# A fused attention and mixer kernel on one core: one group for the last 64 features, denser second sums, v weights on ScalarE's queue, a third band buffer, and a new order

## The chip, the core and the metric

The kernel runs on one core of a Trainium2 chip. A core has five engines that the text names as the profile does: TensorE (PE; PEld is its loading of weights), VectorE (DVE), ScalarE (ACT), GpSimd (POOL) and SyncE (SP). Each engine runs its own instructions strictly in the order in which the program gives them and waits on semaphores for the others. SP here only issues DMA transfers. The metric is the time of one execution on the device in microseconds (us), the median of several runs; less is better. The notes also use one profiled execution, whose span runs from its first to its last instruction.

## What is computed

The input x has 2048 tokens of 448 features. Two blocks follow each other, each on a layer-normalized input and each added to its input; all normalizations have no learned scale.

```python
h  = x + A(layernorm(x), wqkv, wo)
h2 = h + B(layernorm(h), w1, w2, w3, w4)

# A: 16 heads of 28 features; each token attends to itself and the
#    tokens 2, 4, ... 14 before it (8 in all), softmax over these 8
# B: g  = gelu(layernorm(x) @ w1), cut into four groups of 112 features,
#         shifted by +1, -1, +2, -2 tokens
#    x1 = x + g @ w2
#    return x1 + gelu(layernorm(x1) @ w3) @ w4      # w3: 448 -> 1792
```

## The kernel before

The tokens are worked on in four quarters of 512 (t = 0 to 3) and, from the mixer's second product on, in five units u of 2, 4, 4, 4 and 2 tiles of 128 tokens. The steps of a quarter are, with the names of the functions:

- N1 (line 654): statistics and normalization of x. VectorE makes most of it, ScalarE that of quarter 3.
- A1 (line 670): the normalized rows are transposed (by PE in quarters 0 and 1, by a DMA transpose in 2 and 3); then q and k of 3 x 128 features each and of the last 64 features (line 692). The copies out of PSUM (evictions) write `qT`, and `kk` or, for the last 64 features, `kr`, with 16 tokens of the stretch before as a pad in front.
- V (line 719): v, evicted to `vt`, spread by DMAs into bands `vw`.
- A2 (line 742): VectorE multiplies queries with eight shifted copies of the keys, 4096 columns for each of three feature groups and 2048 for the last 64 features ("products"); PE sums them over a head's features into logits.
- S (line 765): softmax over the eight: row maximum, difference, Exp, sum, Ln and Exp, multiplication into `pb`; PE turns `pb`, and the result is evicted to `pt`.
- A3 (line 791): VectorE spreads `pt` over a band `bd_r` (80 x 2048, "band product"), PE multiplies it with `vw`; then O (line 806): the product with wo and the residual.
- B1 (line 837): statistics, normalization, DMA transpose; M (line 850): the product with w1, gelu into `gT`.

The steps of a unit are B2 (line 868: the product with w2 over the shifted groups, "second sums"), T (line 905: normalization, transposes by PE in unit 0 and by DMA in the others), W3 (line 915) and B3 (line 932). W3 makes 14 groups of 128 features for each unit, with gelu on ScalarE, and B3 the product with w4 and the stores.

Most sums over features are made by `duo` (line 459): two outputs at a time, each summed over 64-row halves of the array's rows. At each step a matmul on rows 0 to 63 for one output and one on rows 64 to 127 for the other run as a pair. The function `sums` (line 482) gives one output four upper and three lower halves and the other three and four, so 448 features take seven pair steps ("3.5 passes" of full height an output).

The groups of the mixer have 112 features, so their lower half has only 48 rows. For units 0 and 1 (`DENSE = 2`, line 19) the second sums take four upper and four lower halves an output: eight pair steps. From unit 2 on, seven DMAs a unit (line 874) gather the lower rows densely into `ht`, with w2's rows in the same order in `w2_l` (seven loads, line 964), and seven pair steps do.

The last 64 features of q and k (lines 692 to 705) are summed in quarters of the array, 64 rows by 64 columns: X takes q and Y takes k, with the even tiles of a quarter in the upper 64 partitions of the output and the odd ones in the lower. These are 28 matmuls of 256 columns. Three pads (lines 713 to 716) are copied besides.

The order of the work is written out by hand in a list of numbers, `ORDER` (line 20). Each operation has a number in the order in which the code creates it; `arrange` (line 193) goes through the list, hands out buffers, and appends each operation to its engine's instructions. `OTHER` (line 52) names operations that go to VectorE in place of ScalarE. A transposing DMA waits for the landing of all ordinary DMAs that stand before it in the list, and an ordinary DMA for the transposing one before it (lines 206 to 211). The loads of an engine's queue keep their order (line 452). At the start PE runs `WARM = 11` matmuls on the identity (line 647).

Of the kernel before, what the change touches and what calls it, by code (L numbers as in the profile page):

```python
# [50 lines left out]
"""  # L51
OTHER = """
92 182 483 489 492 495 546 552
"""
FULL = (4,)
FILL = (0, 0, 0, 0)
WARM = 11
# [225 lines left out]
def bass_sequential_preLN__sliding_local_dilated__mixer_s_mlp__prompt_kernel(  # L283
# [18 lines left out]
    LOWER = ((0, 64, 112, 0, 64), (1, 64, 80, 0, 112), (1, 80, 112, 1, 64), (2, 64, 96, 1, 96), (2, 96, 112, 2, 64), (3, 64, 112, 2, 80), (3, 0, 64, 3, 64))  # L302
# [11 lines left out]
    with ExitStack() as es:  # L314
# [14 lines left out]
        w2_s = sb("w2_s", [KC, 4, D], BF16)  # L329
        w2_l = sb("w2_l", [128, 4, D], BF16)  # L330
        ht = sb("ht", [128, 4, 512], BF16)
# [35 lines left out]
        gT = arv(A_QG, KC, 4 * QGW).rearrange("p (c n) -> p c n", c=4)  # L367
        kk = [arv(A_KV + t * KVB, 128, 3 * KVW).rearrange("p (c n) -> p c n", c=3) for t in range(NST)]
        kr = [arv(A_KV + t * KVB + 3 * KVW, 128, 4 * KW).rearrange("p (j n) -> p j n", j=4) for t in range(NST)]
# [5 lines left out]
        def shifted(t, c):  # L375
            return bass.AP(AR, A_KV + t * KVB + c * KVW + PADK, [[A_END, 128], [64, 8] if c < 3 else [KW, 4], [-DIL, NW], [1, 64]])
# [50 lines left out]
        def load_x(i, n):  # L427
            return dma("x%d" % i, xin[:, i:i + n, :], xv[:, i:i + n, :], 128 * n * D * 2)

        def load_rows(chan, dst, src, lo, n):  # L430

            for h in range(2):
                dma("%s%s" % (chan, "ab"[h]), dst[:, 2 * h:2 * h + 2, :], src[192 * h:192 * h + 256, lo:lo + n].rearrange("(c k) n -> k c n", k=128), 256 * n * 2)
# [16 lines left out]
        dma("w2", w2_s[:], B_w2.rearrange("(c k) n -> k c n", k=KC), D * D * 2)  # L450
# [169 lines left out]
        def setup_late(after):  # L620
# [15 lines left out]
            late("memset", ap=kr[0][0:64, 0, 0:PADK], constant=0.0)  # L636
            late("memset", ap=vw[0:PADK, 0, 0, :], constant=0.0)
            late("memset", ap=gT[:, :, 0:2], constant=0.0)
            late("memset", ap=gT[:, :, 2 + SEQ:4 + SEQ], constant=0.0)
# [30 lines left out]
        def phase_A1(t):  # L670
# [37 lines left out]
            def last(lo, h, n):  # L708
                return Y(lambda v: v[64 * h:64 * h + 64, 0:256].rearrange("p (j n) -> p j n", j=4)[:, lo:lo + n, 64 - PADK:])
# [342 lines left out]
```

## Time and profile before

| | |
|---|---|
| median of 3 runs | 189.51 us (188.73 to 191.31) |
| span of the profiled execution | 186.4 us |
| what the median has around that span | 3.1 us |
| PE busy | 180.3 us, 2496 matmuls |
| VectorE busy | 127.0 us |
| ScalarE busy | 122.1 us |
| GpSimd busy | 24.0 us |
| DMA | 18.59 MB, of it 8.14 MB read from HBM |

The profile gives no time of the profiled execution outside of its span. Matmuls overlap, and their ends are modelled, so a busy PE can still contain short waits. Nearly every instruction has the line 1010, where the program emits what was recorded before; so groups are told apart by the names of what is written and read (`ps` is a bank of PSUM, `arena` the memory that q, k, gelu results and the weights wqkv, w3 and w4 share, `w_s` the weights w1 and w2). Times of points are microseconds from the start of the span.

### The profile page before, as it was taken

Reading aid. Unit: us, or ns where it says so; the run is one execution under the profiler, and the core shown is the slowest. Engines: PE = TensorE matmul, PEld = TensorE weight load, DVE = VectorE, ACT = ScalarE, POOL = GpSimd, SP = SyncE. Lnnn points to the kernel's source line nnn. Section 1 sums busy time; section 2 is a strip of 40 time slices with the busy share of each in tenths; the row PEclk is TensorE's granted clock in tenths of the full one; section 3 lists DMA queues with packets and bytes.
Section 4 is the critical chain, followed back from the end, with each engine's and each line's share of the span. In section 5 each row is a group of like instructions: output and inputs, shape, how many; then the busy total and the mean of one; then the engine's idle time right before and its main releaser. Section 6 shows DMA issues by size and latency. Waiting matters only on the chain.

```text
span 186.4 us, 5772 instructions
## 1 busy us (share of the span) xinstructions
PE 180.3 (97%) x2496; PEld 94.0 (50%) x2496; DVE 127.0 (68%) x225; ACT 122.1 (65%) x289; POOL 24.0 (13%) x59
## 2 busy tenths in 40 slices
PE   6899998999999999999999999999999999999994
PEld 2474333445544565765455544554445544555663
DVE  6799999999999999999476587614087274000403
ACT  3549999898999999957959489503833004730340
POOL 4320000000000000425300000170002805000000
PEclk9999999999999999999999999999999999999999
DMA  5999025865515667914360201491111602300121
GB/s 134 356 282 182 16 51 130 198 216 71 144 38 110 115 216 165 307 53 45 73 116 10 58 8 26 88 141 54 29 40 41 116 0 52 106 0 4 49 98 49
DMA packets 33633, 18.59 MB, mean 100 GB/s; under 512 B 21208, under 2 KB 33096, under 8 KB 33608
## 3 DMA queue, kind: packets, MB, share of 16 engines
q1 hardware_dynamic: 33608, 18.23, 41.5%
q8 instruction: 19, 0.31, 0.6%
q14 instruction: 6, 0.05, 0.1%
HBM read 8.14 MB, written 1.84 MB: 54 GB/s over the span
## 4 chain that ended last, share of the span: by engine, by line
PE 79%; DVE 14%; ACT 4%; DMA 1%; issue 0%; SPq 0%
PE ps L1010 79%; DVE qk_r L1010 9%; DVE st L1010 1%; ACT lntm L1010 1%; DMA xin<-in_A_x_dram 1%; DVE lntm L1010 1%; ACT L1010 1%; DVE mx L1010 1%; DVE xin L1010 1%; ACT arena L1010 1%; ACT h3T L1010 1%; DVE pb L1010 0%; DVE ls L1010 0%; DVE mv L1010 0%; ACT rs_x L1010 0%
## 5 line engine op out<-in xcount | busy, mean ns | idle before, releaser
L1010 PE MATMUL ps<-actT,arena 64*128 64x512 bf16 (+2 forms) x812 | 69.8, 326 | 0.9 <-DMA actT<-lntm 0.5
L1010 ACT ACTIVATE h3T<-ps 128x512 bf16<-128x512 f32 (+1 forms) x70 | 30.9, 517 | 38.5 <-PE ps L1010 38.4
L1010 PEld LDWEIGHTS ps<-actT,arena 64*128 64x128 bf16 (+1 forms) x812 | 35.4, 96 | 31.9 <-PE ps L1010 1.9
L1010 PE MATMUL ps<-arena,h3T 64*128 64x448 bf16 (+3 forms) x434 | 44.9, 343 | 0.2
L1010 ACT ACTIVATE arena<-ps 128x512 bf16<-128x512 f32 (+6 forms) x66 | 30.7, 508 | 8.5 <-PE ps L1010 8.1
L1010 PEld LDWEIGHTS ps<-arena,h3T 64*128 64x128 bf16 (+1 forms) x434 | 22.6, 94 | 20.0 <-ACT h3T L1010 0.6
L1010 DVE TENSOR_TENSOR qk_r<-arena 128x4096 bf16<-128x4096 bf16 (+1 forms) x16 | 31.9, 2013 | 0.1
L1010 DVE SCALAR_TENSOR_TENSOR qk_r<-ps,mrs,arena 128x448 bf16<-128x448 f32 (+2 forms) x17 | 10.4, 651 | 30.9 <-PE ps L1010 30.9
L1010 POOL TENSOR_TENSOR arena<-arena,xin 128x448 f32<-128x448 f32 x16 | 16.1, 1035 | 77.9 <-ACT lntm L1010 65.5
L1010 DVE TENSOR_TENSOR bd_r<-arena,bmask 80x2048 bf16<-80x2048 bf16 x16 | 19.0, 1214 | 1.7 <-PE ps L1010 1.7
L1010 DVE SCALAR_TENSOR_TENSOR arena<-xin,rs_y,ps 128x448 f32<-128x448 bf16 x16 | 10.3, 671 | 11.0 <-PE ps L1010 11.0
L1010 PE MATMUL ps<-wo_s,actT 64*128 64x448 bf16 x128 | 14.5, 350 | 0.1
L1010 PE MATMUL ps<-actT,w_s 64*112 64x512 bf16 x112 | 13.4, 379 | 0.0
L1010 PE MATMUL ps<-w_s,arena 64*128 64x448 bf16 x83 | 12.8, 349 | 0.1
L1010 PE MATMUL ps<-arena,actT 64*128 64x448 bf16 x112 | 12.3, 351 | 0.2
L1010 ACT ACTIVATE actT<-ps 128x512 bf16<-128x512 f32 (+2 forms) x19 | 11.7, 639 | 1.1 <-PE ps L1010 1.0
L1010 ACT ACTIVATE lntm<-xin,nm 128x448 bf16<-128x448 bf16 x16 | 10.6, 672 | 1.1 <-DVE nm L1010 1.1
L1010 DVE BATCH_NORM_STATS2 st<-xin 128x6 f32<-128x448 bf16 x16 | 9.2, 614 | 1.0 <-DMA xin<-in_A_x_dram 0.9
L1010 PEld LDWEIGHTS ps<-actT,w_s 64*112 64x112 bf16 x112 | 7.2, 126 | 4.4 <-ACT arena L1010 0.3
L1010 ACT ACTIVATE rs_x<-mv,epsilon 128x4 f32<-128x4 f32 (+2 forms) x16 | 4.6, 298 | 6.4 <-DVE mv L1010 6.3
L1010 PEld LDWEIGHTS ps<-w_s,arena 64*128 64x128 bf16 x83 | 5.5, 95 | 6.1 <-PE ps L1010 0.5
L1010 ACT ACTIVATE vt<-ps 128x448 bf16<-128x448 f32 x16 | 8.3, 546 | 0.5 <-PE ps L1010 0.5
(73 smaller groups left out, 161.6 us busy)
## 6 DMA issues: line engine op xcount, KB each, us to landing
arena<-in_B_w_dram SPq DMA_DIRECT2D x2, 896.0 KB, 5.9
out_dram<-qk_r SPq DMA_DIRECT2D x15, 112.0 KB, 1.8
arena<-in_B_w_dram SPq DMA_DIRECT2D x2, 784.0 KB, 7.3
vw<-vt SPq DMA_DIRECT2D x4, 320.0 KB, 4.3
vw<-vt SPq DMA_DIRECT2D x4, 256.0 KB, 4.1
arena<-in_A_wqkv_dram SPq DMA_DIRECT2D x2, 448.0 KB, 4.7
xin<-in_A_x_dram SPq DMA_DIRECT2D x2, 448.0 KB, 7.5
xin<-in_A_x_dram SPq DMA_DIRECT2D x3, 224.0 KB, 5.5
```

Of the source, the lines that this page charges most:

```text
L1010: inst = getattr(eng, meth)(**kw)
```

## The change

1. *Last 64 features.* A weight tile `wl` holds the last 64 features of q and of k beside each other; GpSimd copies it together once (`setup_last`). Each half of a quarter (256 tokens) is one output of 128 features, and a `duo` sums the two halves: 14 matmuls of 256 columns in the place of 28. The heads' tokens in `kr`, the logits, `pb` and `pt` are laid out by halves instead of even and odd tiles. Four copies of 64 partitions x 256 take the place of two of 128 x 256, and one pad copy that of two.
2. *Second sums.* All units use seven pair steps. Features 64 to 111 of the last group are split over rows 112 to 127 of the other three, by three DMAs a unit (`low`), and the odd tiles' first 64 features of the last group go to the lower half (`odd`, one DMA a unit). w2 is loaded in that arrangement by four loads; `w2_l` and its seven loads go.
3. *Loads.* The v weights are issued on ScalarE's queue and stand first in the list of its loads. On SP x4-5 goes ahead of the second half of the q and k weights.
4. *Buffers and start.* Three band buffers in place of two. Quarter 0's q and k take the 512 tokens in one piece, no longer in two of 256. `WARM` is 7, and one such matmul stands behind each of the first two transposes (`FILL`).
5. *Order.* `ORDER` and `OTHER` are new. What it says around the points that are spoken of here:
   - VectorE, ahead of quarter 0's first product: all four statistics and three aggregates of quarter 2's x (before, two statistics, and the others between the products); both reductions to `bmask` ahead of the first statistics.
   - ScalarE at the start: the v loads after the third transposition copy, then the evictions q0, k0, a row sum of tile 13, q1, k1, q2, k2, the two k halves, quarter 1's two transposition copies, four v evictions, the two q halves, an Ln and an Exp, the pad.
   - SP after quarter 1's DMA transpose: four DMAs of unit 0, one of v, four of unit 1, the second half of w3, w4. Before: the second half of w3, one of v, six of `w2_l`, two of v, w4.
   - PE: the phases follow each other much as before; within them many pairs are exchanged.

```diff
-NQK, NBD, NLN, NACT, NSM, NO = 3, 2, 2, 4, 1, 6
+NQK, NBD, NLN, NACT, NSM, NO = 3, 3, 2, 4, 1, 6
-DENSE = 2
 ORDER = """
-8 9 2 10 12 0 1 39 40 41 42 43 44 45 46 47 48 49 13 5 14 4 15 16 6 33 7 50 17 18 29 51 36 37 34 30 52 55 53 54 56 62
+32 2 36 5 33 8 0 39 6 35 9 1 10 14 15 16 34 43 44 45 17 7 18 50 55 51 52 19 53 46 62 56 60 47 57 48 54 49 63 58
...
-FILL = (0, 0, 0, 0)
-WARM = 11
+FILL = (1, 1, 0, 0)
+WARM = 7
...
+        for h in range(2):
+            load_half("wv", wqkv_s[:, :, 2 * D:3 * D], A_wqkv, 2 * D, D, h, "act")
         act(zs[:, 0, 0:1], epsilon[:, 0:1], ACT.Exp)
-        load_rows("wqk", wqkv_s[:, :, 0:2 * D], A_wqkv, 0, 2 * D)
+        load_half("wqk", wqkv_s[:, :, 0:2 * D], A_wqkv, 0, 2 * D, 0)
         load_x(4, 2)
+        load_half("wqk", wqkv_s[:, :, 0:2 * D], A_wqkv, 0, 2 * D, 1)
         load_x(6, 2)
-        load_rows("wv", wqkv_s[:, :, 2 * D:3 * D], A_wqkv, 2 * D, D)
...
-        dma("w2", w2_s[:], B_w2.rearrange("(c k) n -> k c n", k=KC), D * D * 2)
+        dma("w2a", w2_s[0:KC, 0:3, :], B_w2[0:3 * KC].rearrange("(c k) n -> k c n", k=KC), 3 * KC * D * 2)
+        dma("w2b", w2_s[KC:128, 0:3, :], B_w2[3 * KC + 64:4 * KC].rearrange("(c k) n -> k c n", k=16), 48 * D * 2)
+        for h in range(2):
+            dma("w2%s" % "cd"[h], w2_s[64 * h:64 * h + 64, 3, :], B_w2[3 * KC:3 * KC + 64, :], 64 * D * 2)
...
+        def setup_last():
+            pool("tensor_copy", out=wl[:].rearrange("p c (g n) -> p c g n", g=2),
+                 in_=wqkv_s[:, :, D - 64:3 * D - 64].rearrange("p c (g n) -> p c g n", g=2)[:, :, :, 0:64])
...
-                duo(A, B, ((0, 256), (256, 256)) if t == 0 else ((0, 512),), after=filled if t == 0 else ())
+                duo(A, B, ((0, 512),), after=filled if t == 0 else ())
...
-            copy(qT[:, 3, now:now + 256], X(lambda v: v[:, 0:256]))
-            copy(kr[t][:, :, PADK:], Y(lambda v: v[:, 0:256].rearrange("p (j n) -> p j n", j=4)), False)
-            copy(kr[t][64:128, :, 0:PADK], last(0, 0, 4), False)
-            copy(kr[t][0:64, 1:4, 0:PADK], last(0, 1, 3), False)
+            ends = []
+
+            def half(h):
+                b = _Tile(P_bank)
+                ends.append(b)
+                return sums(lambda lo, n: b(lambda v: v[:, 0:256].rearrange("p (i n) -> p i n", i=2)),
+                            lambda c, part: wl[part, c, :],
+                            lambda c, part, lo, n: rows(a, c, 2 * h, 2, part), h == 0)
+
+            duo(half(0), half(1), ((0, 256),))
+            for h, b in enumerate(ends):
+                copy(qT[64 * h:64 * h + 64, 3, now:now + 256], b(lambda v: v[0:64, 0:256]))
+                copy(kr[t][64 * h:64 * h + 64, PADK:], b(lambda v: v[64:128, 0:256]), False)
+            copy(kr[t][64:128, 0:PADK], ends[0](lambda v: v[64:128, 256 - PADK:256]), False)
...
-            if dense:
-                for c, lo, hi, k, at in LOWER:
-                    dma("ht", ht[at:at + hi - lo, k, 0:n], gT[lo:hi, c, 2 + first + SHIFT[c]:2 + first + SHIFT[c] + n], (hi - lo) * n * 2)
+            for c in range(3):
+                dma("low%d" % u, gT[KC:128, c, 2 + first + SHIFT[c]:2 + first + SHIFT[c] + n], gT[64 + 16 * c:80 + 16 * c, 3, 2 + first + SHIFT[3]:2 + first + SHIFT[3] + n], 32 * n)
+            dma("odd%d" % u, ht[BOT, tiles[0] // 2:tiles[0] // 2 + len(tiles) // 2, :],
+                gT[TOP, 3, 2 + first + SHIFT[3]:2 + first + SHIFT[3] + n].rearrange("p (i n) -> p i n", n=256)[:, :, 128:], 64 * n)
...
-                if dense:
-                    top = side(TOP, range(3 + upper))
-                    bot = [(ht[BOT, k, 128 * i - first:128 * i - first + 128], (lambda lo, m, k=k: w2_l[BOT, k, lo:lo + m])) for k in range(4 - upper)]
-                else:
-                    top, bot = side(TOP, range(4)), side(slice(64, KC), range(4))
+                top, bot = side(TOP, range(3 + upper)), side(BOT, range(3))
+                if not upper:
+                    bot.append((ht[BOT, i // 2, :], lambda lo, m: w2_s[BOT, 3, lo:lo + m]))
```

More of the change, by code (lines that the diff above doesn't have):

```diff
@@ L328, in bass_sequential_preLN__sliding_local_dilated__mixer_s_mlp__prompt_kernel @@
         w1_s = sb("w1_s", [128, 4, D], BF16)
-        w2_s = sb("w2_s", [KC, 4, D], BF16)
-        w2_l = sb("w2_l", [128, 4, D], BF16)
-        ht = sb("ht", [128, 4, 512], BF16)
+        w2_s = sb("w2_s", [128, 4, D], BF16)
+        wl = sb("wl", [128, 4, 128], BF16)
+        ht = sb("ht", [128, NTL // 2, 128], BF16)
         ident = sb("ident", [128, 128], BF16)
@@ L366, in bass_sequential_preLN__sliding_local_dilated__mixer_s_mlp__prompt_kernel @@
         qT = arv(A_QG, 128, 4 * QGW).rearrange("p (c n) -> p c n", c=4)
-        gT = arv(A_QG, KC, 4 * QGW).rearrange("p (c n) -> p c n", c=4)
+        gT = arv(A_QG, 128, 4 * QGW).rearrange("p (c n) -> p c n", c=4)
         kk = [arv(A_KV + t * KVB, 128, 3 * KVW).rearrange("p (c n) -> p c n", c=3) for t in range(NST)]
-        kr = [arv(A_KV + t * KVB + 3 * KVW, 128, 4 * KW).rearrange("p (j n) -> p j n", j=4) for t in range(NST)]
+        kr = [arv(A_KV + t * KVB + 3 * KVW, 128, PADK + 256) for t in range(NST)]
         pt = [arv(A_KV + t * KVB + 4 * KVW, KW, 1024) for t in range(NST)]
@@ L427, in load_x, with load_half @@
         def load_x(i, n):
-            return dma("x%d" % i, xin[:, i:i + n, :], xv[:, i:i + n, :], 128 * n * D * 2)
+            dma("x%d" % i, xin[:, i:i + n, :], xv[:, i:i + n, :], 128 * n * D * 2)
+        def load_half(chan, dst, src, lo, n, h, eng="sp"):
+            dma("%s%s" % (chan, "ab"[h]), dst[:, 2 * h:2 * h + 2, :], src[192 * h:192 * h + 256, lo:lo + n].rearrange("(c k) n -> k c n", k=128), 256 * n * 2, eng)
         def load_rows(chan, dst, src, lo, n):
             for h in range(2):
-                dma("%s%s" % (chan, "ab"[h]), dst[:, 2 * h:2 * h + 2, :], src[192 * h:192 * h + 256, lo:lo + n].rearrange("(c k) n -> k c n", k=128), 256 * n * 2)
+                load_half(chan, dst, src, lo, n, h)
         S.tag = "load"
@@ L635, in setup_late @@
             late("memset", ap=kk[0][:, :, 0:PADK], constant=0.0)
-            late("memset", ap=kr[0][0:64, 0, 0:PADK], constant=0.0)
+            late("memset", ap=kr[0][0:64, 0:PADK], constant=0.0)
             late("memset", ap=vw[0:PADK, 0, 0, :], constant=0.0)
-            late("memset", ap=gT[:, :, 0:2], constant=0.0)
-            late("memset", ap=gT[:, :, 2 + SEQ:4 + SEQ], constant=0.0)
+            late("memset", ap=gT[0:KC, :, 0:2], constant=0.0)
+            late("memset", ap=gT[0:KC, :, 2 + SEQ:4 + SEQ], constant=0.0)
+        def setup_last():
+            pool("tensor_copy", out=wl[:].rearrange("p c (g n) -> p c g n", g=2),
+                 in_=wqkv_s[:, :, D - 64:3 * D - 64].rearrange("p c (g n) -> p c g n", g=2)[:, :, :, 0:64])
         busy = _Tile(P_bank)
@@ L688, in phase_A1 @@
                 (A, ev_a), (B, ev_b) = group(k, names[k], True), group(k + 1, names[k + 1], False)
-                duo(A, B, ((0, 256), (256, 256)) if t == 0 else ((0, 512),), after=filled if t == 0 else ())
+                duo(A, B, ((0, 512),), after=filled if t == 0 else ())
                 ev_a()
                 ev_b()
-            X, Y = _Tile(P_bank), _Tile(P_bank)
-            both = ((X, D - 64, ((0, 1, 2, 3), (0, 2, 3))), (Y, 2 * D - 64, ((0, 1, 3), (0, 1, 2, 3))))
-            op = None
@@ L695, in phase_A1 @@
-            for second in range(2):
-                turned = [op] * second
-                specs = []
-                (bu, wu, cu), (bl, wl, cl) = both[::-1] if second else both
-                for n, (ct, cb) in enumerate(zip(cu[0], cl[1])):
-                    for e in range(2):
-                        for b, w, c, part in ((bu, wu, ct, TOP), (bl, wl, cb, BOT)):
-                            specs.append((e, dict(out=b(lambda v, e=e: v[64 * e:64 * e + 64, 0:256].rearrange("p (i n) -> p i n", i=4)),
-                                                  lhsT=wqkv_s[part, c, w:w + 64], rhs=a(lambda v, e=e, c=c, part=part: v[part, :, c, 64 * e:64 * e + 64]),
-                                                  start=not second and n == 0, stop=bool(second) and n == 2), 256))
-                op = S.group("pe", [("matmul", kw) for _, kw, _ in specs], pe=[(n, "s", None) for _, _, n in specs])
-                op.sdeps.update(turned)
@@ L715, in phase_A1 @@
+            duo(half(0), half(1), ((0, 256),))
[3 more added lines that the diff above has]
+            copy(kr[t][64:128, 0:PADK], ends[0](lambda v: v[64:128, 256 - PADK:256]), False)
             if t + 1 < NST:
-                copy(kr[t + 1][0:64, 0:1, 0:PADK], last(3, 1, 1), False)
+                copy(kr[t + 1][0:64, 0:PADK], ends[1](lambda v: v[64:128, 256 - PADK:256]), False)
@@ L755, in phase_A2 @@
                     for j in range(4):
-                        lo = (2 * j + e if c < 3 else j) * 512
+                        lo = (4 * e + j) * 512
                         terms.append((L(lambda v, j=j: v[32 * j:32 * j + 32, :].rearrange("p (r j x e) -> p j x r e", r=NW, j=4, x=NW)),
@@ L783, in turn @@
                 part = (TOP, BOT)[h]
-                return (h, dict(out=banks[h](lambda v: v[0:KW, 64 * r:64 * r + 64]), lhsT=pb[part, sl, r * KW:(r + 1) * KW], rhs=ident[part, part],
+                return (h, dict(out=banks[h](lambda v: v[0:KW, 64 * r:64 * r + 64].rearrange("p (e j n) -> p j e n", e=2, j=2)), lhsT=pb[part, sl, r * KW:(r + 1) * KW], rhs=ident[part, part],
                                 start=True, stop=True), 64)
@@ L788, in phase_A2 @@
             for h, b in enumerate(banks):
-                copy(pt[t].rearrange("p (n r) -> p n r", r=NW)[:, 64 * h:64 * h + 64, :], b(lambda v: v[0:KW, :].rearrange("p (r n) -> p n r", r=NW)))
+                copy(pt[t].rearrange("p (e h n r) -> p e h n r", e=2, h=2, r=NW)[:, :, h, :, :], b(lambda v: v[0:KW, :].rearrange("p (r e n) -> p e n r", r=NW, e=2)))
         def phase_A3(t):
@@ L797, in phase_A3 @@
                 dve("tensor_tensor", block=True, out=bd(lambda v: v.rearrange("p (n g r) -> p n g r", g=8, r=NW)),
-                    in0=pt[t][:, il * 256:il * 256 + 256].rearrange("p (n r) -> p n r", r=NW).unsqueeze(2).broadcast_to([KW, 32, 8, NW]),
-                    in1=bmask[:].rearrange("p (g r) -> p g r", r=NW).unsqueeze(1).broadcast_to([KW, 32, 8, NW]), op=ALU.mult)
+                    in0=bass.AP(pt[t].tensor, pt[t].offset + 32 * il * NW, [list(pt[t].ap[0]), [NW, 32], [0, 8], [1, NW]]),
+                    in1=bass.AP(bmask, 0, [[64, KW], [0, 32], [NW, 8], [1, NW]]), op=ALU.mult)
                 mms([(b(lambda v, j=j, lo=128 * c + 64 * a2: v[32 * j:32 * j + 32, lo:lo + 64]),
@@ L855, in group @@
                             lambda c, part, lo, n: rows(a, c, 0, 4, part), upper), \
-                    lambda: act(gT[:, g, 2 + t * 512:2 + (t + 1) * 512], b(lambda v: v[0:KC, :]), ACT.Gelu_apprx_tanh)
+                    lambda: act(gT[0:KC, g, 2 + t * 512:2 + (t + 1) * 512], b(lambda v: v[0:KC, :]), ACT.Gelu_apprx_tanh)
             for g in (0, 2):
@@ L962, in load_w4 @@
         def load_w4():
-            for c, lo, hi, k, at in LOWER:
-                low = dma("w2l", w2_l[at:at + hi - lo, k, :], B_w2[KC * c + lo:KC * c + hi, :], (hi - lo) * D * 2)
-                low.odeps.add([op for op in S.ops if op.tag == "load" and op.is_dma][-1])
             w4_v = B_w4.rearrange("(f k) n -> k f n", k=128)
@@ L972, in bass_sequential_preLN__sliding_local_dilated__mixer_s_mlp__prompt_kernel @@
         setup()
+        setup_last()
         S.tag = "warm"
```

8 lines of the change are left out of this document (2 added, 6 removed), and 59 rows, old and new, of the table ORDER.

## Prediction

> **What bounds the kernel now.** I read the page first, then busy time by stretch, then the chain that ended last, then each engine's timeline around the points that the change touches.
>
> ```profile
> span 186.4 us, 5772 instructions
> PE 180.3 (97%) x2496; PEld 94.0 (50%) x2496; DVE 127.0 (68%) x225; ACT 122.1 (65%) x289; POOL 24.0 (13%) x59
> ```
>
> Read alone, 97% says that TensorE (PE) is the bound everywhere. The stretches say otherwise (columns: elapsed, then busy us and instructions of PE, weight loads, VectorE, ScalarE, GpSimd, then clock and DMA):
>
> ```profile
> 0.00:14.28 14.28, 12.04 (x153) 7.03 (x155) 11.31 (x33) 7.01 (x18) 4.47 (x35) 1.00 0.90 257
> 14.28:74.80 60.52, 59.44 (x999) 27.98 (x996) 60.41 (x75) 58.51 (x151) 0.00 (x0) 1.00 0.57 127
> 74.80:115.70 40.90, 40.53 (x638) 22.12 (x632) 31.08 (x67) 31.95 (x71) 7.63 (x11) 1.00 0.32 75
> 115.70:184.00 68.30, 68.24 (x714) 36.84 (x714) 23.83 (x51) 24.65 (x52) 11.94 (x13) 1.00 0.26 59
> ```
>
> From 14.28 to 74.80 VectorE is idle 0.1 us of 60.5, ScalarE 2.0; PE's busy time there has small waits under its modelled ends. The chain agrees:
>
> ```profile
> 14.28 2.29 DVE qk_r L1010
> 76.64 11.72 PE ps L1010 x190
> 115.72 68.26 PE ps L1010 x714
> ```
>
> ```profile
> 74.81 0.51 DVE L1010 TENSOR_SCALAR lntm<-arena,nm,rs_y 128x448 bf16<-128x448 f32 x1
> 72.38 3.20 PE L1010 MATMUL ps<-w_s,arena 64*128 64x448 bf16 x32
> ```
>
> 14.28 is the first query-key product of quarter 0. VectorE goes on without a pause to the first normalization of unit 0 (74.81), whose transposes, behind unit 1's second sums (72.38) in PE's order, release the first W3 matmul (76.64); from there PE always has work. So the kernel is a VectorE part, then a PE part: an edit before 76.64 pays if it brings that matmul forward, one after it pays if it takes PE time. In both orders VectorE has the same 105 operations ahead of unit 0's first normalization, with two swapped for equals, and PE the same phases ahead of the first W3 matmul, but for the pieces, fills and warm matmuls that the diff changes. The new order can therefore move that point only by waits, not by work.
>
> **What PE can still gain after 76.64.** The same forms, between 76.6 and 115.7 (first two rows) and between 115.7 and 179 (last two):
>
> ```profile
> L1010 PE MATMUL ps<-actT,arena 64*128 64x512 bf16 x98 | 11.7, 376 | 0.0
> L1010 PE MATMUL ps<-wo_s,actT 64*128 64x448 bf16 x64 | 7.1, 350 | 0.1
> L1010 PE MATMUL ps<-arena,h3T 64*128 64x448 bf16 x308 | 30.8, 349 | 0.1
> L1010 PE MATMUL ps<-actT,arena 64*128 64x512 bf16 x196 | 21.8, 376 | 0.0
> ```
>
> Two half-height matmuls run as a pair: 11.7/49 = 0.239 us against 21.8/98 = 0.222 late; 7.1/32 = 0.222 against 30.8/154 = 0.200. The excess is 0.8 and 0.7 us; with some 0.6 for the smaller groups I put what a better order could win there at 2.1 us.
>
> **Mixer's second sums in 3.5 passes.** Seven pair steps instead of eight for each of the three tile pairs of units 0 and 1: 3 x 0.200 = 0.6 us of PE. All three lie ahead of 76.64, where VectorE sets the time, so I count 0; ends -0.6 and 0. If VectorE were not full there, the 0.6 would count whole.
>
> **Last 64 features as one group.** Both ways make seven passes over 256 columns; 28 quarter matmuls become 14 half ones a quarter.
>
> ```profile
> L1010 PE MATMUL ps<-actT,arena 64*64 64x256 bf16 x112 | 4.6, 276 | 0.2
> L1010 PE MATMUL ps<-actT,arena 64*128 64x256 bf16 x280 | 17.5, 269 | 0.1
> L1010 ACT ACTIVATE arena<-ps 128x256 bf16<-128x256 f32 x8 | 2.9, 392 | 0.0
> L1010 ACT ACTIVATE arena<-ps 64x64 bf16<-64x64 f32 x4 | 0.9, 216 | 0.1
> L1010 POOL TENSOR_TENSOR arena<-arena,xin 128x448 f32<-128x448 f32 x16 | 16.1, 1035 | 77.9 <-ACT lntm L1010 65.5
> ```
>
> PE: 4.6/4 = 1.15 us a quarter now, 7 x 0.125 = 0.88 then; 1.1 us in all, again under VectorE: 0. ScalarE pays: two copies of 256 columns become four of half the partitions. No row has 64x256; 128x256 and 64x64 bound it (0.39 and 0.22). I take the end with the same columns, 0.39. Two pads of about 0.22 become one. Net 0.78 - 0.22 = +0.56 us a quarter, 2.2 in all, against ScalarE's 2.0 idle between 14.28 and 74.80. These copies stand ahead of the Exp, Ln and eviction steps that VectorE's products and row sums wait for, so the engine's slack is about used up; still VectorE had none of those waits to speak of, so I take a tenth of it, +0.2; ends 0 and +1.2 (a little over half). GpSimd joins the weights once: 512 columns at most at its sum's 1.04 us for 448 are 1.2 us, from the landing of the weights near 8.7 to about 10; the group needs them after 21 pair steps of 0.23, some 5 us after the first matmul, so 0.
>
> **The start.** Now the key weights' second half and the v weights go ahead of later x tiles; then x4-5 goes ahead of that half, and the v weights leave this queue.
>
> ```profile
> 8.13 5.88 PE L1010 MATMUL ps<-actT,arena 64*128 64x256 bf16 x106
> 5.34 1.16 SPq L1010 DMA_DIRECT2D xin<-in_A_x_dram  x2
> xin<-in_A_x_dram SPq DMA_DIRECT2D x2, 448.0 KB, 7.5
> 7.82 0.42 DVE L1010 COPY actT<-ps 128x512 bf16<-128x512 bf16 x1 [0.19 <-PE ps L1010]
> 8.71 2.21 DVE L1010 BATCH_NORM_STATS2 st<-xin 128x6 f32<-128x448 bf16 x4 [0.46 <-DMA xin<-in_A_x_dram]
> 11.80 1.31 DVE L1010 TENSOR_SCALAR lntm<-xin,mv,rs_y 128x448 bf16<-128x448 bf16 x4 [0.30 <-ACT rs_y L1010]
> 19.75 0.37 DVE L1010 BATCH_NORM_AGGREGATE mv<-st 128x2 f32<-128x6 f32 x4
> ```
>
> x4-5 is waited for until 8.71. One 448 KB load less ahead of it, at the first stretch's 257 GB/s, is 1.8 us: 6.9; VectorE, with both mask reductions now ahead of its first statistics, gets there at about 7.2. From there the new order has, ahead of the first product, 8 statistics (2.21/4 = 0.55), 6 normalizations (0.33), 7 aggregates (0.09) and one copy (0.42): 4.4 + 2.0 + 0.6 + 0.4 = 7.4, so it starts near 14.6, 0.3 later; but two statistics and three aggregates (1.3 us) are by then behind it, not between products. Net -1.0; ends -1.8 and 0 (0 if x8-11 comes no earlier). The first matmul then waits for all four tiles, hence for VectorE's copy, which stands behind two more statistics: near 9.2 instead of 8.13. Eleven pair steps of 0.23 and two evictions of 0.53 later, at 12.8, the first product could start; VectorE comes at 14.6, so nearly 2 us cover the later start.
>
> [...] No row here has two queues loading at once.
>
> Part of the gain is given back. In ScalarE's new order the pad copy that the fourth product needs stands behind six evictions, a row sum that needs x12-15, two transposition copies and all v evictions.
>
> ```profile
> 11.67 1.07 ACT L1010 ACTIVATE arena<-ps 128x512 bf16<-128x512 f32 x2
> 15.82 1.94 ACT L1010 ACTIVATE actT<-ps 128x1024 bf16<-128x1024 bf16 x2
> 18.57 0.98 ACT L1010 ACTIVATE vt<-ps 128x448 bf16<-128x448 f32 x2
> 20.16 0.30 ACT L1010 ACTIVATE rs_x<-mv,epsilon 128x4 f32<-128x4 f32 x1
> ```
>
> From the first eviction at 9.2 + 11 x 0.23 = 11.7: 6 x 0.53, 0.5 for the row sum (448 columns, as a v eviction) and up to 0.8 waiting for x12-15 (issued at 5.9 now, 7.5 to landing), 4 x 0.3 small copies, 1.9, 4 x 0.49, 0.5, 0.2: 22.0. VectorE is there at 14.6 + 3 x 2.2 + 0.1 = 21.3. Hence +0.6 (ends 0 and +1.5). What is late next is the row maximum of quarter 0, behind the same product. The v weights, in spite of the change's words, are not first in time: ScalarE issues them after its third transposition copy, near 8.6; V's matmuls, which follow the query-key matmuls (now until 8.13 + 5.88 = 14.0), cover that.
>
> **SP's queue before W3.** All units now copy gelu rows by DMA, four issues each. Units 0 and 1 put eight, and one v copy, between quarter 1's transpose and the second half of w3, which now follows it directly.
>
> ```profile
> 65.61 0.39 SPq L1010 DMA_DIRECT2D arena<-in_B_w_dram  x1
> 66.05 0.79 SPq L1010 DMA_DIRECT2D vw<-vt  x1
> 66.88 3.21 SPq L1010 DMA_DIRECT2D w_l<-in_B_w_dram  x6
> arena<-in_B_w_dram SPq DMA_DIRECT2D x1, 896.0 KB, 5.3
> arena<-in_B_w_dram SPq DMA_DIRECT2D x2, 784.0 KB, 7.3
> 64.90 6.08 ACT L1010 ACTIVATE arena<-ps 112x512 bf16<-112x512 f32 x13
> ht<-arena SPq DMA_DIRECT2D x1, 64.0 KB, 2.5
> ```
>
> At 3.21/6 = 0.54 an issue, 8 x 0.54 + 0.79 = 5.1 us. Unit 1's four also wait for a gelu of quarter 1, the ninth of the 13, near 69.3. Two things then wait that did not. Unit 1's sums, at 72.38 now, need copies that land 2.5 after an issue at 70.7 to 71.5: 73.2 to 74.0; behind them in PE's order stand unit 0's transposes, and so W3. And w3's half goes out near 71.5 and lands 5.3 later at 76.8, against 76.64 for the matmul that needs it; now it lands at 70.9, so 5.7 us of cover is gone. Behind it SP holds the w4 halves, which the first B3 sums need, well after W3's. The two waits run side by side: 0 to 1.4, and 0.2. PE comes to those sums a little later too, since unit 0's also wait (65.6 + 4 x 0.54 + 2.5 = 70.3). I take +0.5; ends 0 and +2.2 (7.3 to landing as the w4 halves). The 21 `ht` and 7 `w_l` DMAs that go stood beside full engines: 0.
>
> **Third band buffer, new order.** VectorE waits once for a band buffer:
>
> ```profile
> 100.46 2.36 DVE L1010 TENSOR_TENSOR bd_r<-arena,bmask 80x2048 bf16<-80x2048 bf16 x2 [1.73 <-PE ps L1010]
> ```
>
> VectorE is not the bound there; the 1.7 reach PE only through its gaps. With the rest of the order I take -0.3; ends -2.1 and +2.1.
>
> **Sum.** -1.0 + 0.6 + 0.2 + 0.5 - 0.3 = 0.0 us. The span stays 186.4; the median of the runs, 189.5, lies 3.1 above it, which I take for what is around the span: **189.5**.
>
> **Rivals.** (1) *Gains stand*: no product waits for ScalarE and the order closes three quarters of the late gaps: -1.0 - 1.6, **186.9**, at best 185.0 (all of 1.8, 2.1 and the second sums' 0.6). For: one visible wait goes. Against: ScalarE is as full as VectorE. (2) *The start runs slow*: warm-up has 7 matmuls, not 11, then a hole until the first transposes.
>
> ```profile
> 1.63 4.61 PE L1010 MATMUL ps<-ident 128*128 128x512 bf16 x11 [1.63 <-POOL mhalf L1010]
> ```
>
> 4.61/11 = 0.42 us for 512 columns is twice the 0.22 seen later, through the fills' 4.2 us; yet the clock column says 1.00. If seven fills (2.9 us) don't end that, the first 4.2 us of query-key matmuls run at half speed, 2.1 us of PE; past 2 us of cover, evictions and pad copy pass on about 1.5: **191.0**. The two fills between transposes speak against. [...] (3) *w3 decides*: nine issues at the v copy's 0.79 end at 72.7; with 7.3 to landing, 80.0. PE's order has only W3 matmuls there, so each us past 76.64 counts: +3.4, **192.9**; at 1.0 an issue 194.7.
>
> **Chances.** Forecast 0.55 (own range 188.2 to 191.0), (1) 0.17, (2) 0.13, (3) 0.15. Low 186.0 and high 193.4 leave out the ends of (1) and (3), less than 0.2. A measurement of this kernel tells about 2% from no change, 185.7 to 193.3: faster 0.08 (nearly half of 1), slower 0.12 (over half of 3, and 2 with 3), same 0.80.
>
> **What would show it.** Right: VectorE full from about 14.6 to 75, first W3 matmul at 76 to 77, PE full afterwards. Wrong: a VectorE wait over 1 us between products; W3's first matmul waiting for a DMA; query-key pairs at 0.43 us; PE gaps after 77 other than now.

## The result and the profile after

The changed kernel takes 201.01 us (median; 199.86 to 203.36) where the kernel before takes 190.41 beside it: the ratio is 1.0565, 95% interval 1.0471 to 1.0658. The prediction was 189.5 with 186.0 to 193.4, no change. The profiled execution took 199.91 us, its span is 198.2, so 11.8 us more than before's 186.4.

Busy time by stretch, after (columns as in the prediction):

```profile
0.00:14.08 14.08, 10.59 (x63) 4.94 (x65) 12.20 (x38) 6.74 (x17) 5.19 (x37) 1.00 0.91 255
14.08:53.00 38.92, 36.58 (x664) 17.40 (x661) 35.55 (x39) 37.35 (x98) 0.00 (x0) 1.00 0.49 116
53.00:56.50 3.50, 0.03 (x1) 0.00 (x0) 3.50 (x2) 2.18 (x8) 0.00 (x0) 0.80 0.39 116
56.50:62.00 5.50, 5.49 (x32) 2.60 (x33) 0.27 (x1) 1.19 (x5) 0.00 (x0) 0.51 0.01 3
62.00:84.94 22.94, 21.48 (x285) 10.40 (x283) 20.79 (x32) 21.51 (x49) 0.20 (x1) 1.00 0.38 82
84.94:126.00 41.06, 40.11 (x638) 24.10 (x636) 29.95 (x64) 31.52 (x70) 5.42 (x7) 1.00 0.35 92
```

The first product starts at 14.08 (14.28 before), unit 0's first normalization at 84.94 (74.81 before): the second point moves by 10.1 us. Of the 11.8 us, 10.3 are lost between the two points and 1.7 behind them, and 0.2 are gained ahead of them. VectorE, which was idle 0.1 us between them, is now idle 10.7. Its longest waits (in total, times, longest):

```profile
DVE nmr L1008 <- ACT rs_y L1008: 5.3, 1, 5.3
DVE qk_r L1008 <- ACT arena L1008: 2.5, 2, 2.3
DVE bd_r L1008 <- ACT arena L1008: 0.7, 2, 0.4
DVE arena L1008 <- PE ps L1008: 0.5, 1, 0.5
DVE qk_r L1008 <- PE ps L1008: 0.5, 1, 0.5
DVE lntm L1008 <- ACT rs_y L1008: 0.5, 1, 0.5
```

The 2.3 stand ahead of quarter 0's fourth product (23.06), the 5.3 in quarter 0's B1 (62.09), where VectorE multiplies the means with `rs_y`, the reciprocal standard deviations. The second has its origin on PE. The Ln and Exp that make this `rs_y` stand in ScalarE's order behind a residual copy of quarter 1's output projection (into `xin`), and ScalarE waits 5.6 us for PE ahead of that copy:

```profile
ACT xin L1008 <- PE ps L1008: 5.8, 2, 5.6
```

PE's timeline there (start, length, in brackets the idle time before):

```profile
51.93 0.92 PE L1008 MATMUL ps<-wo_s,actT 64*128 64x448 bf16 x8
52.68 0.35 PE L1008 MATMUL ps<-xin,ident 64*128 64x448 bf16 x1
56.51 0.53 PE L1008 MATMUL ps<-xin,ident 64*128 64x448 bf16 x1 [3.47 <-issue]
56.51 2.02 PE L1008 MATMUL ps<-wo_s,actT 64*128 64x448 bf16 x8
```

PE stops for 3.47 us between the two halves of one pair, in the middle of a group, where the program puts no wait; the profile has only "issue" for it. Then the same eight matmuls take 2.02 us instead of 0.92: the granted clock in the table row from 56.50 to 62.00 is 0.51, where it was 1.00 up to 53.00 and is 1.00 again from 62.00 on. VectorE comes out of this 5.3 us late, through ScalarE's order.

What did PE wait for? The DMA queues and issues from 46.8 to 54.25 (columns of a queue: packets, MB, share of the engines; of an issue: KB each, us to landing):

```profile
q1 hardware_dynamic: 854, 1.45, 64.8%
...
arena<-in_B_w_dram SPq DMA_DIRECT2D x1, 896.0 KB, 7.1
```

and in the 0.2 us from 54.25:

```profile
q8 instruction: 1, 0.02, 30.0%
```

From 46.8 to 54.25 the DMA engines carry the band copies of v of quarters 2 and 3 and, issued at 48.04, the 896 KB of w3's first half, but no fetch of instructions starts. At 54.33, with that load nearly through (it lands 7.1 us after its issue, at 55.1), one 16 KB fetch starts; it takes 0.96 us, and 1.2 us later PE goes on. This half of w3 was issued at 35.58 before; the new order puts it between the band copies of quarter 2.

### The profile page after: what moved, and what is told of

Read it like the earlier page. It is cut to its first block, busy times and chain, and to the rows that moved or that the text cites. A ratio compares the mean times of both kernels' runs of the same rounds, so it can differ in the third digit from the quotient of the medians.

```text
span 198.2 us, 5580 instructions
## 1 busy us (share of the span) xinstructions
PE 183.2 (92%) x2390; PEld 96.1 (49%) x2390; DVE 128.1 (65%) x224; ACT 128.8 (65%) x296; POOL 24.7 (12%) x60
## 4 chain that ended last, share of the span: by engine, by line
PE 68%; ACT 14%; DMA 11%; issue 3%; DVE 3%; SPq 1%
PE ps L1008 68%; ACT arena L1008 5%; DMA arena<-in_A_wqkv_dram 4%; ACT lntm L1008 3%; DMA arena<-in_B_w_dram 3%; DMA actT<-lntm 2%; DMA xin<-in_A_x_dram 1%; ACT vt L1008 1%; SPq L1008 1%; ACT L1008 1%; ACT h3T L1008 1%; ACT rs_x L1008 1%; DVE xin L1008 1%; DVE st L1008 1%; DVE nm L1008 0%
## 5 line engine op out<-in xcount | busy, mean ns | idle before, releaser
L1008 PE MATMUL ps<-actT,arena 64*128 64x512 bf16 (+1 forms) x658 | 66.9, 347 | 1.6 <-ACT actT L1008 0.6
L1008 PEld LDWEIGHTS ps<-actT,arena 64*128 64x128 bf16 x658 | 32.2, 95 | 31.0 <-PE ps L1008 2.5
L1008 ACT ACTIVATE arena<-ps 128x512 bf16<-128x512 f32 (+4 forms) x70 | 32.7, 506 | 7.9 <-PE ps L1008 7.2
L1008 PEld LDWEIGHTS ps<-arena,h3T 64*128 64x128 bf16 (+1 forms) x434 | 23.1, 94 | 20.0 <-ACT h3T L1008 1.0
L1008 PE MATMUL ps<-wo_s,actT 64*128 64x448 bf16 x128 | 17.3, 391 | 0.7 <-ACT h3T L1008 0.6
L1008 PE MATMUL ps<-actT,w_s 64*112 64x512 bf16 x112 | 14.2, 380 | 1.2 <-ACT arena L1008 1.1
L1008 ACT ACTIVATE actT<-ps 128x512 bf16<-128x512 f32 (+2 forms) x20 | 12.3, 640 | 1.2 <-PE ps L1008 1.1
L1008 PEld LDWEIGHTS ps<-wo_s,actT 64*128 64x128 bf16 x128 | 7.2, 103 | 11.1 <-issue 6.7
L1008 POOL TENSOR_TENSOR mrs<-nm,rs_y 128x4 f32<-128x4 f32 x4 | 0.8, 200 | 82.5 <-ACT rs_y L1008 81.3
L1008 DVE TENSOR_SCALAR lntm<-arena,mv,rs_y 128x512 bf16<-128x512 f32 x14 | 6.8, 544 | 3.7 <-POOL rs_y L1008 3.1
```

The source lines that it names most:

```text
L1008: inst = getattr(eng, meth)(**kw)
```

## Experiments

Ratios are those to the kernel before, on the same chip, with 95% intervals. Operations of `ORDER` are named by number and by what they do.

### The stop on PE: load, instructions, or the order

**w3's first half where it was before** (behind quarter 1's last band copy of v):

```diff
-446 445 30 365 366        # 30: w3, first half
+446 445 365 366
-153 148 242 149 150       # 242: quarter 1, last band copy
+153 148 242 30 149 150
```

> Only the load of w3's first half (896 KB) moves on SP's queue: directly behind quarter 1's last band copy of v, as before the change, instead of between quarter 2's first two. Fetch theory: TensorE ran dry at 53.0 because the fetch of its next block of instructions stood behind this load and the band copies around it (fetch seen only at 54.3), and the 3.5 us without matmuls then halved its granted clock for some 5 us. Without the load there, both go: VectorE's 5.3 us wait for the rs_y of quarter 1's B1 falls under 1 us, no 3 us piece called issue is left in the chain near 53, span 198.2 becomes 192 to 194, time 201.0 becomes 194 to 196.5. Order theory: the stop belongs to the new order of PE's work around quarter 1's output projection (something that the profile doesn't name); a load that PE needs only at 87 moves nothing, hole and time stay, 200 to 201.5.

1.0306 (1.0239 to 1.0373), median 194.95. Its trace, PE at the same place, and the fetch, in the 0.2 us from 50.5:

```profile
52.08 0.92 PE L1017 MATMUL ps<-wo_s,actT 64*128 64x448 bf16 x8
52.84 0.55 PE L1017 MATMUL ps<-xin,ident 64*128 64x448 bf16 x2
53.04 1.10 PE L1017 MATMUL ps<-wo_s,actT 64*128 64x448 bf16 x8
```

```profile
q8 instruction: 1, 0.02, 36.6%
```

No stop, a granted clock of 1.00 from 50 to 62, the fetch at 50.6 instead of 54.3, and unit 0's first normalization at 78.82, 6.1 us earlier; the span is 192.1, also 6.1 less. (The B1 that had waited is quarter 0's, which the expectation calls quarter 1's.)

**More instructions ahead, same load and order.**

```diff
             for n in range(WARM):
-                keep_busy()
+                if n < 4:
+                    keep_busy()
+                else:
+                    b = busy(lambda v: v[0:32, 0:32])
+                    mms([(b, ident[:, 0:32], ident[:, 0:32], True, True, 32, None)] * 27)
```

> Of the seven warm-up matmuls of 512 columns, three become 27 each of 32 weights by 32 columns: 78 matmuls more, so 156 TensorE instructions more ahead of everything, nothing else changed (order, DMA, waits stay). Fetch theory: blocks of instructions are fetched every 256 instructions, so each fetch is asked for 156 instructions earlier in the work: the one that came at 54.3 would be asked for when PE stands at its instruction of 45.5 instead of about 48.9, ahead of the 896 KB load; the hole at 53 to 62 goes though TensorE has more to do; 194 to 197. Order theory: 201 to 203, hole unchanged, plus what the extra matmuls cost at the start.

1.0363 (1.0308 to 1.0417). PE has 156 instructions more, the load stands where the change put it, and the stop is gone: the granted clock from 53 to 66 is 1.00. The fetch comes at 49.46 (the 0.2 us from 49.4), ahead of the load, which is issued at 50.77 here:

```profile
q8 instruction: 1, 0.02, 34.2%
```

**256 instructions more:** as the last edit, with `n < 1` and 23, 23, 22, 22, 22, 22 small matmuls.

> The kernel after, with 128 TensorE matmuls (256 instructions with their weight loads) more in the warm-up: six of the seven 512-column ones become 134 small ones. Fetch theory with blocks of 256 instructions: the block borders fall at the same places of the work as in the kernel after, w3's first half still loads at 48, so the hole of 3 to 4 us at some 53 and the half clock behind it come back, 200 to 203. If more instructions as such, or a changed start, took the hole away in the kernel with 156 more: 194.5 to 197, no hole.

1.0624 (1.0537 to 1.0711), and the stop is back, between the same two matmuls:

```profile
54.27 0.92 PE L1012 MATMUL ps<-wo_s,actT 64*128 64x448 bf16 x8
55.02 0.35 PE L1012 MATMUL ps<-xin,ident 64*128 64x448 bf16 x1
58.78 0.53 PE L1012 MATMUL ps<-xin,ident 64*128 64x448 bf16 x1 [3.41 <-issue]
```

The profile of this run counts one fetch more than that of the changed kernel, which has 19 for 4780 matmuls and weight loads, one for every 252 (before: 19 for 4992, one for every 263):

```profile
q8 instruction: 20, 0.33, 0.7%
```

So neither the load alone nor the order alone stops PE, nor more instructions as such: with 0 and with 256 more it stops, with 156 more it does not, which fits a step of 252 to 263 instructions from fetch to fetch. That PE needs the instructions of the fetch behind the load, and that this fetch was asked for earlier and stood in line, is an inference from its start at the load's end; the trace shows no request.

**The kernel before with the late load:** `27` (w3, first half) moved from behind 431 to behind 357 (quarter 2's first band copy).

> The kernel before, with the load of w3's first half moved to where the change puts it, directly behind quarter 2's first band copy of v (issue near 48.5 instead of 35.6). Fetch theory: the harm needs a block border within the load; before's fetches stand at 48.2 and 54.8, so the load falls between two of them: 189 to 190.5, no hole. If the load harms there by itself (it delays the band copies, or takes from PE what it reads): 192 to 196.

1.0026 (0.9994 to 1.0057), no stop. One fetch stands at 48.47, ahead of the load's issue at 48.98, the next at 55.73, in the load's last microsecond, and PE does not run dry in between: it is busy 12.93 of the 13.00 us from 53 to 66. The same late load cost nothing that shows here, with a fetch just ahead of it.

### The v weights

```diff
-load_half("wv", ..., D, h, "act")
+load_half("wv", ..., D, h)            # SP, between x6-7 and x8-11
```

> The v weights go back to SP's queue, between x6-7 and x8-11 as before the change; all else as after. If their landing at 17.3 (8.4 us after the issue, behind the output and mixer weights) is what delayed V of quarter 0, and with it the evictions that stand ahead of the pad copy for the fourth product: V's first eviction at about 18.5 instead of 19.7, VectorE's wait ahead of the fourth product 2.25 falls to about 1, time 201.0 becomes 199 to 200.5 with the hole at 53 still there (unless the fetch shifts against the load). If the v weights are covered, as the prediction had it: no change, 200.5 to 201.5; x8-15 then land up to 1.5 later and the first product moves from 14.1 towards 15.

1.047 (1.0401 to 1.0539): a little better than the change, though the intervals overlap. The stop is still there in the profiled execution, 4.4 us long. But one of the four runs had a mean granted clock of 1.00 and took 196.85 us, where the others had 0.98, so the stop may have been missing in it, and the small gain need not come from the v weights.

With w3's first half early as well:

> w3's first half early and the v weights on SP's queue, both as before the change, the rest as after. Fetch theory with late v weights: the two gains add, 192.5 to 195.5. If both theories fall: 200 to 201.5. If it comes to the 190.4 of before or less, these two placements are the whole loss; if it stays at 193 or more, about 2 us or more belong to the rest of the change (ScalarE's extra copies, the order after 62).

1.0292 (1.0239 to 1.0344) against 1.0306 with w3 alone: nothing. PE no longer waits for v weights, but in this run the first product came at 15.37 and the fourth still waited 1.7 us.

### Quarter 0's wait

All of these have w3's first half early. **Pad copy early:**

```diff
-315 210 122 ... 119 121 120 111 113 26 ... 75 115 419
+315 111 113 115 210 122 ... 119 121 120 26 ... 75 419
# 111, 113: last 64 q; 115: pad; 210: transposition copy; 120, 121: evictions of V
```

> The kernel with w3's first half early, and in ScalarE's order of quarter 0 the two query copies of the last 64 features and the pad copy go directly behind the two key copies, ahead of quarter 1's two transposition copies and V's four evictions; nothing else changes. If ScalarE's order alone makes VectorE wait 2.2 us for the fourth product: the pad copy ends near 18.4 instead of 23.0, that wait falls under 0.3, the first product of quarter 1 comes at 25.2 to 25.8 instead of 27.5, and the time falls by 1.7 to 2.4, from 194.95 to 192.5 to 193.3. If ScalarE is simply full, V's evictions and the copies behind them are late instead: the wait moves to the row maximum or to quarter 1's products, and the time falls by less than 0.7.

1.0187 (1.012 to 1.0255): lower than 1.0306, with intervals that just overlap. But the wait is not gone. The waits of VectorE from 14 to 35:

```profile
DVE qk_r L1017 <- PE ps L1017: 2.5, 1, 2.5
```

The profile names the later of two releasers. With the pad copy out of the way it shows the other: a product buffer (there are three), free only when PE has summed the first product, which PE does behind V, and V waits 1.51 us for its weights. The next run tests this.

**Sums of the first products ahead of V on PE** (129, 131 ahead of 122; 133, 135 behind 119), on top of the pad copy:

> The kernel with w3 early and the pad copy early, and in PE's order the mask row and the sums of quarter 0's first product go ahead of V's matmuls of quarter 0, those of the second and third product directly behind them; GpSimd's small memsets that they need go ahead as well. Buffer theory: VectorE's 2.5 us wait for the fourth product is for a product buffer (there are three), which is free only when PE has summed the first product, and PE does that behind V, which waits 1.5 us for its weights. With the sums ahead, the fourth product starts near 21 instead of 23.25, its wait falls under 0.6, and the time falls by 1.5 to 2.3, from 194.1 to 191.8 to 192.6. If quarter 1's first products then wait for their query and key copies, which go behind these sums on PE: less than 1 is left, 193.1 to 194.

1.0183 (1.0085 to 1.0281), no gain over 1.0187 that this interval could show.

**v weights issued behind ScalarE's first transposition copy** (11, 12 behind 88), with the pad copy early and without that edit:

> The kernel with w3 early and the pad copy early, and ScalarE issues the two v weight loads behind its first transposition copy instead of its third, about 1.2 us earlier. Buffer theory: V's matmuls start 0.8 to 1.5 earlier, the sums of the first product too, the wait for the fourth product falls from 2.5 to 1.0 to 1.7, time 192.6 to 193.4. If the v weights only take their share from x8 to x15 (both queues load at once then): V is earlier but the first product is later by up to 1, and the time stays at 193.7 to 194.5.

1.0296 (1.0233 to 1.0358): nothing gained, and the fourth product still waits 2.35 us. Both edits together gave 1.0226 (1.0101 to 1.0351).

**11 warm-up matmuls again**, with the pad copy early:

```diff
-                keep_busy()
+                mms([(busy(), ident[:], ..., True, True, 512, None)] * (2 if n < 4 else 1))
```

> The kernel with w3 early and the pad copy early, with the warm-up at 11 matmuls of 512 columns as before the change, not 7 (the two fills between transposes stay). Cold start theory: in the changed kernels the first 42 query-key matmuls take 4.7 to 7.0 us from run to run, as TensorE's clock is at half for part of them, and the first product slips from 14.0 to as much as 16.2; four more warm-up matmuls (1.7 us, into the idle 1 to 1.5 us ahead of the first transposes) make it 4.7 in each run: first product near 14, median 194.1 becomes 193.0 to 193.6 and the runs lie closer together. If the slips come from the x loads alone: 194 to 195, as before this edit.

1.0184 (1.013 to 1.0239): no effect beside 1.0187. With the sums ahead of V:

> As the run above, with the mask row and the first product sums ahead of V in PE's order too. Buffer theory and cold start theory: 191.5 to 192.8. If VectorE only waits elsewhere in quarter 0 (the run without the warm-up had 1.3 us for a ScalarE copy sum in place of the 2.5 for the buffer): 192.8 to 194.

1.0212 (1.0167 to 1.0257). The fourth product no longer waits here (20.41); in its place, from 14 to 35:

```profile
DVE nm L1017 <- ACT lntm L1017: 1.3, 1, 1.3
DVE lntm L1017 <- ACT rs_y L1017: 0.4, 1, 0.4
```

The kernel before with seven full warm-up matmuls (`if n < 7: keep_busy()`, else 32 by 32):

> The kernel before, with four of its 11 warm-up matmuls cut to 32 weights by 32 columns, so seven of full length are left. Cold start theory: the query-key matmuls of quarter 0 (4.3 us for the 84 of 128 rows that are warm now) take up to 2 us more in some runs, and the time goes from 189.8 to 190.2 to 191.2. Else: 189.5 to 190.2.

1.0022 (0.9988 to 1.0056): the shorter warm-up isn't the loss.

**ScalarE's row sums, with an Ln and an Exp, ahead of V's evictions** (318, 319, 419, 422, 421 ahead of 125), with the pad copy early, the sums ahead of V and seven warm-up matmuls:

> The kernel with w3 early, the pad copy early and the first product sums ahead of V, and in ScalarE's order N1's logarithm and exponential for tiles 8 to 11 and the three row sums of x12, x14 and x15 ahead of V's four evictions. Wandering wait theory: with the sums ahead, the wait for a product buffer (2.5 us) was replaced by waits of 1.3 for these row sums and 0.4 to 0.6 for the exponential; ahead of V's evictions, where ScalarE is idle 0.9 us waiting for V, both go, and the time falls by 1 to 1.8 against the kernel with the sums ahead alone (1.018 to 1.021 of the kernel before): 1.010 to 1.014, 192.0 to 192.8. If ScalarE is full in quarter 0: V's evictions are then later by 2, the next wait is for banks or for V, and the ratio stays at 1.017 to 1.022.

1.0284 (1.0241 to 1.0326). The wait is now for the row maximum:

```profile
DVE mx L1017 <- PE ps L1017: 2.5, 1, 2.5
```

**The fourth product's sums ahead of quarter 1 on PE** (136, 137 behind 135), on top of the last edit:

> As the last kernel (w3 early, pad copy early, the first sums and the row sums of x12 to x15 ahead of V's matmuls and evictions), and the sums of the fourth product directly behind those of the second and third in PE's order, ahead of quarter 1's last 64 features and first query-key group. In the last kernel VectorE's only long wait was 2.5 us for the row maximum of quarter 0, which needs these sums. Wandering wait theory: row maximum at about 22.7 instead of 25.25, first product of quarter 1 at 25 instead of 27.2 unless its copies are late, ratio to before falls from 1.028 to 1.012 to 1.018. ScalarE-is-full theory: the wait goes on to quarter 1's query and key copies and the first normalization of unit 0 stays where it was, near 79; ratio 1.022 to 1.030.

1.032 (1.027 to 1.037). Row maximum at 23.00, but the first product of quarter 1 waits:

```profile
DVE qk_r L1017 <- ACT arena L1017: 3.1, 1, 3.1
```

**Four of ScalarE's evictions to VectorE** (120, 121, 214, 215 added to `OTHER`), on top of the last edit, with quarter 0's row maximum and subtraction (138, 139) moved ahead of the last two:

> As the last kernel, and four of ScalarE's evictions go to VectorE, into its 3.1 us wait of quarter 0: two of V's of quarter 0 and the first query and key group of quarter 1 (some 1.9 us off ScalarE, 0.7 each on VectorE). The row maximum and the subtraction of quarter 0 go ahead of the latter two. ScalarE-is-full theory: from the first product to unit 0's first normalization each kernel took ScalarE's busy time plus 2 to 4 us (before 58.5 and 60.5; the kernel with the pad copy early 62.1 and 64.3); with 1.9 less on ScalarE the stretch falls to 63 to 64 from 65.7 in the last kernel, ratio from 1.032 to 1.015 to 1.024. If it is the order of waits alone, VectorE gets 2.8 us more to do and is late by what it did not wait: ratio 1.028 to 1.036.

1.0318 (1.0267 to 1.037): no change from the last. VectorE's waits from 14 to 35 fall to 1.3 us in all, but it has 2.4 us more to do, and the first normalization of unit 0 stays at 80.1.

### ScalarE's copies

```diff
-copy(qT[..., now:now + 256], ...)              # and kr alike, with the pad copy early
+S.group("act", [("activation", ...128 columns...) for m in range(0, 256, 128)])
```

> The kernel with w3 early and the pad copy early, and each of ScalarE's 16 copies of 64 by 256 (last 64 features of q and k) split in two of 128 columns: about 0.18 us more each by the rows 64x64 at 0.216 and 64x256 at 0.378, together some 2.9 us more of ScalarE, about what the change added to it. The prediction's price, a tenth of what ScalarE gets more: +0.2 to +0.5. If ScalarE has no slack left: +1.5 to +2.9.

1.0242 (1.017 to 1.0314) against 1.0187 (1.012 to 1.0255): inconclusive. The dose was also smaller than planned: 6.8 us for the 32 pieces against 5.9 for the 16 copies, as neighbouring pieces overlap (32 of 0.266 would be 8.5).

```profile
L1017 ACT ACTIVATE arena<-ps 64x128 bf16<-64x128 f32 x32 | 6.8, 266 | 0.3
```

## Why the prediction was wrong

The picture of the bound held: a VectorE part up to unit 0's first normalization, then a PE part, and the new order could move that point only by waits. It moved by 10.1 us, and VectorE's busy time up to it did not grow (60.1 us from the first product, 60.4 before): all of it is waits.

**The step that failed** is the term "third band buffer, new order": -0.3, ends -2.1 and +2.1. Its bounds came from one band wait at 100 and from PE's gaps behind 77. It did not ask what the order does to the transfers ahead of 75. The prediction followed w3's second half past eight gelu copies and did not look at the first half, which moves from 35.6 to 48.0, into band copies. A row for what that meets stands on the page of before, and no term was made of it:

```profile
q8 instruction: 19, 0.31, 0.6%
```

Where the prediction had -0.3, moving that one load back gives 6.1 us (198.2 to 192.1 in the profiled spans; the ratios, 1.0565 and 1.0306, put it at some 4.9 of 190): 3.5 of stop, and 2.6 behind it, which fits the lower clock (5.5 us at 0.51 lose 2.7).

**The start, -1.0 and +0.6.** The first product came at 14.08, even ahead of the 14.6 forecast, and the pad copy ended at 22.96, against 22.0. But it was no gain: the statistics taken out from between the products left VectorE at the fourth product at 20.8, where PE's first sums and the pad copy end at 22.8 to 23.0 whatever VectorE does. The wait was 2.25 us, not 0.7. "V's matmuls cover that" failed too:

```profile
17.40 2.83 PE L1008 MATMUL ps<-arena,actT 64*128 64x448 bf16 x28 [1.33 <-DMA arena<-in_A_wqkv_dram]
```

The loads went out at 8.45 and 8.90, as forecast, but the second took 8.4 us to land; SP had by then issued the output and first mixer weights. The first packet of ScalarE's queue starts at 12.3, and from there to 16.8 packets of the two queues alternate; that SP's transfers held the v weights up is an inference from this. The prediction, without a row of two queues loading at once, took the landing to be covered. Yet giving the weights their old place gained nothing that shows: with w3 early the fourth product then waited 1.7 us for a copy of ScalarE's.

**ScalarE's copies, +0.2.** A copy of 64 by 256 took 0.378 us, close to the 0.39 taken. Before, ScalarE was busy 58.5 us from the first product to unit 0's first normalization; with w3 early it was busy 62.3, which is 3.8 more where the term had 2.2 more, and the stretch is 64.7 instead of 60.5:

```profile
14.16:78.82 64.66, 61.26 (x983) 29.81 (x981) 59.94 (x72) 62.31 (x157) 0.20 (x1) 1.00 0.51 105
```

VectorE's work is much the same (59.9 after 60.4), so ScalarE stands closest to the limit there now. Whether the 3.8 set the time was not shown: in the experiment with four evictions taken off it, ScalarE is busy 60.2 us there and the stretch is 66.0.

**w3's second half, +0.5.** In the chain that ended last:

```profile
81.33 5.64 DMA arena<-in_B_w_dram
...
87.02 5.21 PE ps L1008 x92
```

PE's first W3 matmul waits for that half; the cover went as forecast. From unit 0's first normalization to that matmul it took 2.08 us, 1.83 before, so it cost some 0.3. **The second sums at 0** and the last 64 features on PE at 0 were not tried alone.

**The rivals.** Gains stand: no. A slow start: there is one in some runs, but the number of warm-up matmuls does not decide it: with seven the kernel before stays at 1.0022, at most 1.0056. w3 decides: it did, by its first half and not by the issue times of the second.

**What stays open.** The one load accounts for about half of the loss. With w3 early and the pad copy early the kernel is still at 1.0187, some 3.5 us over before. About 1.5 of that, by the trace with w3 early, lie behind the first W3 matmul. There PE has the same work and waits more. With w3 early, from the first W3 matmul on, then before's:

```profile
80.89:189.70 108.81, 107.04 (x1290) 59.71 (x1290) 53.55 (x113) 57.84 (x121) 18.14 (x21) 1.00 0.26 60
```

```profile
76.64:184.00 107.36, 106.98 (x1290) 58.03 (x1290) 53.15 (x114) 54.76 (x118) 18.68 (x24) 1.00 0.27 61
```

Two waits for gelu results, in the trace with w3 early, make most of it:

```profile
87.42 0.93 PE L1017 MATMUL ps<-wo_s,actT 64*128 64x448 bf16 x8 [0.66 <-ACT h3T L1017]
...
121.03 4.15 PE L1017 MATMUL ps<-arena,h3T 64*128 64x448 bf16 x42 [0.61 <-ACT h3T L1017]
```

The other 2 us belong to quarters 0 to 2. Five edits each took away the wait that VectorE showed (pad copy, product buffer, row sums, row maximum, most of that for quarter 1's copies), and each time one of 1 to 3 us stood at the next place. Whether another order ends that, or PE, ScalarE and VectorE are together at their limit there, the runs do not say. None of the kernels beats the one before.

## What to carry to other kernels

If an engine stops in the middle of a group, with nothing named that it waits for, look for a fetch of the instruction queue behind a large load. Here the 896 KB load was issued at 48.04, the fetch started at 54.33 and PE stood still for 3.47 us; with the load moved, the stop was gone. 156 instructions more took the stop away and 256 brought it back, with the load where it was, so an edit elsewhere in the program decided whether the load did harm: 1.0363 without the stop, 1.0624 with it. And a wait is worth its length only if nothing else is due at the same place: look for the second releaser before a move is booked as a gain.

## What the runs showed of the hardware

- The profile counts the fetches of instructions as a queue of its own (q8), as a share of the same 16 DMA engines as data. The kernel after has 19 of them, 16 KB each, for 4780 matmuls and weight loads (all other engines together have 800 instructions), 252 to a fetch; that they are PE's is an inference from these counts. 156 instructions more removed the stop, 256 brought it back with one fetch more. The one fetch that came late cost 5 to 6 us here.

```profile
q8 instruction: 19, 0.31, 0.7%
```

- The stop of 3.47 us cost more than itself: the granted clock was 0.51 for the 5.5 us behind it.
- The start differs between executions by 2 us, though the warm-up is the same. The first 42 query-key matmuls, in two kernels with the same 11 warm-up matmuls (the one with the pad copy early, and the one with the sums ahead of V):

```profile
10.48 6.34 PE L1017 MATMUL ps<-actT,arena 64*128 64x512 bf16 x42 [0.57 <-ACT actT L1017]
```

```profile
8.94 4.71 PE L1017 MATMUL ps<-actT,arena 64*128 64x512 bf16 x42 [0.57 <-DVE mv L1017]
```

The first product followed at 15.82 and at 13.77. The mean granted clock of the profiled execution was 0.991 in the first and 1.000 in the second. The six runs of the first kernel split in the same way: three with a mean granted clock of 1.00 took 193.5 to 193.8 us, three with 0.99 took 195.6 to 197.3. The granted clock does not tell every slow start: with seven warm-up matmuls the 42 took 5.96 us at a granted clock of 0.81 from 8 to 17 in the kernel with the sums ahead of V and the v weights earlier, and 6.99 us at 1.00 in the one with the sums ahead of V alone. So differences under 1% between these kernels need many runs.
